# A linear-attention and MLP kernel: the order of norms in layer 0's first stage, and where four small loads are issued

## The chip, the core and the metric

The kernel runs on one core of a Trainium2 chip. The metric is the device time of one execution in microseconds (us); lower is better. The core has five engines with a queue of instructions each: TensorE (PE in the profile; PEld is its weight load, which overlaps the matmuls), VectorE (DVE), ScalarE (ACT), GpSimd (POOL) and SyncE (SP). Each engine takes its own queue strictly in order, and engines wait for each other through semaphores. In this kernel every DMA is issued from SP, so SP's queue is also the order in which transfers start: one transfer that must wait holds back all that stand behind it.

## The reference

Two layers, each a linear-attention block and a gelu MLP, both with a residual. All data is float32; S = 2048 rows, D = 448, 16 heads of 28, F = 1792.

```python
phi = lambda t: jnp.where(t > 0, t + 1, jnp.exp(t)) + 1e-6
pq, pk = phi(q), phi(k)                        # q, k, v = layernorm(x) @ wqkv
kv = jnp.einsum("bhsd,bhse->bhde", pk, v)
z = jnp.einsum("bhsd->bhd", pk)
num = jnp.einsum("bhqd,bhde->bhqe", pq, kv)
den = jnp.einsum("bhqd,bhd->bhq", pq, z)[..., None] + 1e-6
x = x + (num / den) @ wo
x = x + gelu(layernorm(x) @ w1 + b1) @ w2 + b2     # and both lines once more
```

Since kv and z are sums over all rows, the keys of all 2048 rows have to be through before the first row of the attention's output can be made.

## The kernel before

**Tiles.** The 2048 rows are 16 tiles of 128 rows. Products keep float32 accuracy by a split: each operand is rounded to a high part, the rest is a low part, and three matmuls (high by high, high by low, low by high) add up in one PSUM bank. That is why one projection of one tile is 11 matmuls of 448 columns, and why each tile needs a high part (ACT copies: `XH`, `xnh`, `kh`) and a low part (DVE or POOL subtracts: `XL`, `xnl`, `kl`).

**The first stage of a layer** (`phase1`, line 547) runs steps t = 1 to 15 in layer 0 (tile 0 and part of tile 1 are done in `launch`). A step is a string of tokens, read from left to right; the string is the order in which instructions enter the engines' queues, since the kernel writes its own schedule. The tokens stand for:

- `K`, `Q`, `G` (PE): the key projection of tile t, its query projection, and the product of the normed x of tile t-1 with its keys, added up over all tiles. From t = 9 on the queries are left for later, so a step is then 22 matmuls.
- `T`, `X`: tile t+1 turned so that its columns lie on the partitions, and its split. Tiles 0 to 5 are turned by PE (`T`, line 246). Tiles 6 to 15 go by way of DRAM: DVE turns them in squares of 32 (`turn`, lines 277 and 278), SP writes two tiles at a time to DRAM (`store_sq`, line 283) and reads them back in another order with four DMAs (`spread`, line 289); `X` then splits what landed (ACT line 295, DVE line 296).
- `a`, `n`: statistics of a tile (three DVE instructions, lines 193, 199 and 201, and `brs`, a power on POOL, line 203) and the norm itself (DVE line 383). `tu` and `tv` turn it, and after an odd tile store the pair. `sp` reads the pair back, `ld` issues the load of a later tile (line 82).
- `kp`, `kh`, `kl`: phi of the keys (ACT lines 317 and 318, DVE line 320), their high part (ACT line 433), low part and sum (DVE lines 440 and 444). `qp` and `q1` are the same phi for queries, with a store to DRAM (line 462). `s` splits the normed x for `G` (ACT line 415, POOL lines 416 and 417).
- `bg`: the MLP weights w1 and w2 are loaded and split in the background, a piece or two a step. A piece's load on SP (lines 91 to 94 for w1, 349 for w2) goes into one of two staging buffers and waits until POOL has finished with the piece that had the buffer (lines 342, 345, 353).

Which tiles are normed in which step stands in `NORM` (line 507), steps with an order of their own in `STEPS` (line 502).

**Other loads of the first stage.** After step 4 SP loads the biases b1 and b2 (lines 603 and 604), after step 11 wv (`stage_square`, lines 114 to 118), after step 13 wo (`trans_load`, line 616).

**The stage behind it** is written out in `ORDER` (line 494). It first reads back the queries of block 0 (`ld`, line 690: phi(q) from DRAM, and x, line 82), multiplies them with z on POOL (`qz`, line 694), makes kv out of `G` and wv (`kv`, line 641), divides the queries (`qs`, DVE lines 700 to 705), turns them (`tq`, PE line 712) and multiplies kv with wo (`m`, line 651). Query projections that were left over (`Q`) stand between these on PE.

After that come the MLP blocks (`mlp1`, `mlp2`), where PE runs without a break, and layer 1 in the same manner.

Of the kernel before, what the change touches and what calls it, by code (L numbers as in the profile page):

```python
# [22 lines left out]
def linear_attn_mlp_kernel(  # L23
# [15 lines left out]
    S, D = x0.shape  # L39
# [5 lines left out]
    G = 112  # L45
# [235 lines left out]
    def store_sq(key, h):  # L281
        d = stored[key, h] = dram([128, 1024], F32, f"sq_{'_'.join(map(str, key))}_{h}")
        sp.dma_start(d, squares.pop((key, h)))

    def spread(key, h):
        r = spreads[key, h] = half("sp")
        d = stored.pop((key, h)).rearrange("(i r) (m f) -> m r i f", i=4, m=4)
        for m in range(4):
            sp.dma_start(r[m * 32:(m + 1) * 32].rearrange("r (i f) -> r i f", i=4), d[m])
# [66 lines left out]
    bg = bg_pieces()  # L356
# [32 lines left out]
    def stage_t(l, t):  # L389
        if t >= TURNED[l]:  # L390
            turn(xns[l, t], ("a", l, t // 4), t % 4)
            if t % 2:
                store_sq(("a", l, t // 4), t % 4 // 2)

    def stage_sp(l, t):
        if t >= TURNED[l]:
            block(("a", l, t // 4))
            spread(("a", l, t // 4), t % 4 // 2)
# [76 lines left out]
    def stage_g(l, t, acc):  # L475
# [16 lines left out]


    ORDER = (
# [3 lines left out]
    )  # L498
    DEFER = NT - sum(tok in ("Q", "Qa") for tok in ORDER.split())

    STEP = "qp K T X s a kp n kh kl tu tv G bg Q ld sp"
    STEPS = {
# [3 lines left out]
    }  # L506
    NORM = (
        ((2,), (3,), (5, 6), (7,), (8,), (9,), (10,), (11,), (12, 13), (14,), (15,)),
        ((5,), (6,), (7,), (8,), (9,), (10,), (11,), (12, 13), (14,), (15,)),
    )  # L510

# [35 lines left out]
    def phase1(l, tr):  # L547
        za = consts.tile([128, D], F32, name="za", tag="za")
        acc = []
        load_to(l, 4 if l == 0 else NORM[l][1][-1])  # L550
        if l == 0:
            launch(za)
            load_to(l, NORM[l][2][-1])
        for t in range(l == 0, NT):
            norm = NORM[l][t] if t < len(NORM[l]) else ()
            for tok in STEPS.get((l, t), STEP).split():
                if tok[1:].isdigit() and tok[0] in "an":
                    (stage_a if tok[0] == "a" else stage_n)(l, int(tok[1:]))
                elif tok == "q1":
                    stage_qphi(1)  # L560
                elif tok == "sp":
                    for u in norm:
                        if u % 2:
                            stage_sp(l, u)
                elif tok == "ld" and t + 2 < len(NORM[l]):
                    load_to(l, NORM[l][t + 2][-1])
                elif tok == "a":
                    for u in norm:
                        stage_a(l, u)
                elif tok == "n":  # L570
                    for u in norm:
                        stage_n(l, u)
                elif tok == "tu":
                    for u in norm[:1]:
                        stage_t(l, u)
                elif tok == "tv":
                    for u in norm[1:]:
                        stage_t(l, u)
                elif tok == "T" and t + 1 < NT:
                    stage_b(l, t + 1, "acc" if t == 1 else "h")  # L580
                elif tok == "X" and t + 1 < NT and (l == 0 or t + 1 >= 4):
                    stage_x(l, t + 1)
                elif tok == "K":
                    stage_k(l, t)
                elif tok == "qp":
                    stage_qphi()
                elif tok == "kp":
                    stage_kphi(l, t)
                elif tok == "kh":
                    stage_kh(l, t)  # L590
                elif tok == "kl":
                    stage_kl(l, t, za)
                elif tok == "s":
                    stage_s(l, t)
                elif tok == "G" and t >= 1:
                    acc = acc or [bank("acc", 4, f"G{c}")[:, :D] for c in range(4)]
                    stage_g(l, t - 1, acc)
                elif tok == "bg" and l == 0:
                    background(BG[t])
                elif tok == "Q" and t < DEFER:  # L600
                    stage_q(l, t)
            if l == 0 and t == 4:
                sp.dma_start(b1s, b1.rearrange("(c p) -> p c", p=128))
                sp.dma_start(b2b, b2[None, :].to_broadcast([128, D]))
            if t == 11:
                tr.wv = stage_square(wqkv[:, 2 * D:])
            if t == 13:
                trans_load(l, tr)
        return za, acc

# [308 lines left out]
    for l in range(LAYERS):  # L919
        tr = SimpleNamespace(mp={})  # L920
        za, acc = phase1(l, tr)
        if l == 0:
            background(0)
        fill = list(range(DEFER, NT))

        def pre(j):
            for k in range(4):
                load_pq(l, 1, k)
            if l == 0:
                background(2)  # L930

        tok_ = SimpleNamespace(
            Q=lambda j: stage_q(l, fill.pop(0)), Qp=lambda j: fill_qphi(), Qv=lambda j: stage_qphi(j or 9),
            Qa=lambda j: stage_q(l, fill.pop(0), tag="acc"), G=lambda j: stage_g(l, NT - 1, acc),
            ld=lambda j: (load_pq(l, 0, j), load_x(l, j)), z=lambda j: trans_z(tr, za), gt=lambda j: trans_gt(tr, acc),
            kv=lambda j: trans_kv(tr), mask=lambda j: trans_mask(tr), m=lambda j: trans_m(tr, j),
            ms=lambda j: trans_ms(tr, j), qz=lambda j: q_z(l, 0, j, tr), qs=lambda j: q_scale(l, 0, j, tr),
            tq=lambda j: q_transpose(l, 0, j), qq=lambda j: q_split(l, 0, j), o=lambda j: o_mm(l, 0, j, tr),
            la=lambda j: o_ln(l, 0, j), lb=lambda j: o_n(l, 0, j), T=lambda j: m_transpose(l, 0, j),
            x=lambda j: m_split(l, 0, j), tu=lambda j: turn(xns.pop(("m", l, j)), ("m", l, 0), j),  # L940
            st=lambda j: store_sq(("m", l, 0), 0), sp=lambda j: spread(("m", l, 0), 0), pre=pre)
        for tok in ORDER.split():
            name, j = tok.rstrip("0123456789"), int("0" + tok.lstrip("abcdefghijklmnopqrstuvwxyzQTG"))
            getattr(tok_, name)(j)
        assert not fill and not qo
        table(AF.Gelu_apprx_tanh)
        q_z(l, 1, 0, tr)
        mlp1(l, 0, 0)
        trans_chunks(tr)
        for b in range(NB):  # L950
            acc = [bank("acc", 4, f"y{j}")[:, :D] for j in range(4)]
            nxt = b + 1 < NB
            if not nxt and l + 1 < LAYERS:
                st_k = stage_square(wqkv[:, D:2 * D])
                st_q = stage_square(wqkv[:, :D])
                load_to(l + 1, PRE - 1)
            for i in range(NF):
                if i + 1 < NF:
                    mlp1(l, b, i + 1)
                elif nxt:  # L960
                    mlp1(l, b + 1, 0)
                if l == 0 and b == 0 and i:
                    background(1, 1)
                if i == NF - 2 and not nxt and l + 1 < LAYERS:
                    table(AF.Exp)
                if 9 <= i < 13:
                    add_bias(l, b, i - 9)
                if nxt:
                    behind(l, b, i, tr)
                elif l + 1 < LAYERS:  # L970
                    if i == 2:
                        split_kq("k", st_k)
                    if i == 5:
                        split_kq("q", st_q)
                    if i in (3, 4, 6, 7, 8):
                        t = (3, 4, 6, 7, 8).index(i)
                        stage_a(l + 1, t)
                        stage_n(l + 1, t)
                        stage_t(l + 1, t)
                        if t % 2:  # L980
                            stage_sp(l + 1, t)
                    if 9 <= i < 13:
                        stage_x(l + 1, i - 9)
                mlp2(l, b, i, acc)
# [28 lines left out]
```

## Time and profile before

| | |
|---|---|
| time, median of 3 runs | 882.93 us (882.04 to 883.28) |
| the profiled execution | 880.54 us |
| its span, first to last instruction | 878.8 us |
| granted TensorE clock | 1.000 |
| busy, DVE / ACT / POOL | 489.9 / 342.7 / 220.6 us |
| DMA | 95.81 MB, mean 109 GB/s |

The profile gives busy times per engine, the instructions in order of time, a chain of waits that is followed back from a chosen end, and the DMAs. Matmuls are pipelined: one is shown with about 0.37 us while the next starts 0.20 to 0.21 us later, so a stall of PE is read from the distance of two starts and not from its busy time. In the rows, `out<-in` names the tile written and the tiles read; the bracket at a row's end is idle time of the engine just before it and what ended it. `SPq` rows are DMAs at the time when SP issues them. In the chain of waits a DMA's row starts at its issue and lasts until its data has landed.

### The profile page before, as it was taken

The numbers are of one execution on the slowest core, as the hardware profiler recorded it, in microseconds if no ns is written. First come the engines' busy times: TensorE is split into PE (matmuls) and PEld (weight loads), VectorE is DVE, ScalarE is ACT, GpSimd is POOL, SyncE is SP. The second block draws the span as 40 slices with busy tenths as digits, with TensorE's granted clock in tenths as the row PEclk, the third lists the DMA queues.
The fourth block names the chain that finished last, engine by engine and source line by source line (L and its number), as shares of the span: only waits on it lengthen the run. The fifth ranks groups of instructions, "written<-read, shape, count | busy, mean of one in ns | idle before, by whom it ended". The sixth has DMA issues, their size and how long they took to land.

```text
span 878.8 us, 11689 instructions
## 1 busy us (share of the span) xinstructions
PE 872.6 (99%) x4174; PEld 770.4 (88%) x4174; DVE 489.9 (56%) x957; ACT 342.7 (39%) x601; POOL 220.6 (25%) x250
## 2 busy tenths in 40 slices
PE   9999999999999999999999999999999999999998
PEld 8898888888888888888899998888888888888887
DVE  6878586658455544225567875864574473432112
ACT  6666645323223231333355665442233133223221
POOL 5466732325012102012222244220220140140000
PEclk9999999999999999999999999999999999999999
DMA  5476716624312502051135543262332323111001
GB/s 158 136 211 215 228 53 221 189 80 144 132 59 97 163 0 97 1 179 48 48 129 185 168 138 95 97 189 89 104 115 91 123 68 127 49 48 42 1 1 43
DMA packets 64202, 95.81 MB, mean 109 GB/s; under 512 B 8976, under 2 KB 59152, under 8 KB 64144
## 3 DMA queue, kind: packets, MB, share of 16 engines
q1 hardware_dynamic: 64144, 95.06, 34.3%
q8 instruction: 33, 0.54, 0.3%
q14 instruction: 25, 0.20, 0.1%
HBM read 56.70 MB, written 35.13 MB: 104 GB/s over the span
## 4 chain that ended last, share of the span: by engine, by line
PE 89%; DMA 4%; DVE 3%; ACT 1%; SPq 1%; issue 1%; POOL 1%; ACTq 0%; POOLq 0%; DVEq 0%
PE y L821 10%; PE y L820 10%; PE y L819 10%; PE hp L802 9%; PE hp L801 9%; PE hp L803 9%; PE hp L804 3%; PE hp L805 3%; PE psq L308 2%; PE psq L306 2%; PE psq L307 2%; PE op L744 2%; PE op L743 2%; PE op L745 2%; DMA sq_a<-sq 1%; DMA sp<-sq_a 1%
## 5 line engine op out<-in xcount | busy, mean ns | idle before, releaser
L811 DVE TENSOR_TENSOR gl<-g,gh 128x512 fp32r<-128x512 f32 x112 | 82.7, 738 | 300.2 <-ACT gh L810 300.2
L807 ACT ACTIVATE g<-hp,b1s 128x512 f32<-128x512 f32 x112 | 77.1, 689 | 406.5 <-PE hp L805 404.5
L821 PE MATMUL y<-w2h,gl 128*128 128x448 f32 x448 | 163.7, 365 | 0.0
L820 PE MATMUL y<-w2l,gh 128*128 128x448 f32 x448 | 163.6, 365 | 0.0
L819 PE MATMUL y<-w2h,gh 128*128 128x448 f32 x448 | 163.6, 365 | 0.0
L802 PE MATMUL hp<-XH,w1l 128*128 128x512 f32 x336 | 131.5, 391 | 0.0
L801 PE MATMUL hp<-XH,w1h 128*128 128x512 f32 x336 | 131.2, 391 | 0.0
L803 PE MATMUL hp<-XL,w1h 128*128 128x512 f32 x336 | 131.2, 391 | 0.0
L203 POOL TENSOR_TENSOR brs<-bve,mhalf 128x1 f32<-128x1 f32 x64 | 38.9, 609 | 279.1 <-DVE bve L201 275.9
L819 PEld LDWEIGHTS y<-w2h,gh 128*128 128x128 f32 x448 | 84.1, 188 | 9.0
L820 PEld LDWEIGHTS y<-w2l,gh 128*128 128x128 f32 x448 | 84.1, 188 | 8.4
L821 PEld LDWEIGHTS y<-w2h,gl 128*128 128x128 f32 x448 | 84.2, 188 | 6.6
L803 PEld LDWEIGHTS hp<-XL,w1h 128*128 128x128 f32 x336 | 63.1, 188 | 14.3 <-issue 0.6
L802 PEld LDWEIGHTS hp<-XH,w1l 128*128 128x128 f32 x336 | 63.1, 188 | 11.2
L801 PEld LDWEIGHTS hp<-XH,w1h 128*128 128x128 f32 x336 | 63.1, 188 | 10.9
L810 ACT CAST gh<-g 128x512 fp32r<-128x512 f32 x112 | 69.6, 622 | 3.6
L694 POOL TENSOR_TENSOR pz<-pq,zb 128x448 f32<-128x448 f32 x32 | 36.7, 1150 | 83.6 <-DVE dn L700 66.8
L416 POOL TENSOR_TENSOR xnl<-x,xnh 128x384 fp32r<-128x384 f32 x32 | 35.4, 1107 | 76.4 <-ACT xnh L415 48.3
L296 DVE TENSOR_TENSOR XL<-sp,XH 128x512 fp32r<-128x512 f32 x52 | 45.4, 879 | 10.7 <-ACT XH L295 10.7
L805 PE MATMUL hp<-XL,w1x 128*128 128x512 f32 x112 | 43.6, 389 | 0.0
L804 PE MATMUL hp<-XH,w1x 128*128 128x512 f32 x112 | 43.6, 389 | 0.0
L763 POOL TENSOR_TENSOR x<-x,b2b 128x448 f32<-128x448 f32 x32 | 41.9, 1332 | 0.0
(146 smaller groups left out, 1560.5 us busy)
## 6 DMA issues: line engine op xcount, KB each, us to landing
x<-in_A_x_dram SPq DMA_DIRECT2D x32, 224.0 KB, 3.8
pq_d<-eq SPq DMA_DIRECT2D x32, 224.0 KB, 2.9
pq<-pq_d SPq DMA_DIRECT2D x32, 224.0 KB, 3.3
sq_m<-sq SPq DMA_DIRECT2D x14, 512.0 KB, 2.8
sp<-sq_m SPq DMA_DIRECT2D x56, 128.0 KB, 2.9
x<-x_d SPq DMA_DIRECT2D x32, 224.0 KB, 3.3
sq_a<-sq SPq DMA_DIRECT2D x13, 512.0 KB, 2.9
sp<-sq_a SPq DMA_DIRECT2D x52, 128.0 KB, 3.0
```

Source lines behind the costliest of these rows:

```text
L296: eng.tensor_tensor(lo.rearrange("p (c i n) -> p c i n", c=4, n=32), x, f(h), op=OP.subtract)
L801: pe.matmul(o, w1h[:, c, s], x.moving(x.hi, c), start=(c == 0), stop=False)
L802: pe.matmul(o, w1l[:, c, s], x.moving(x.hi, c), start=False, stop=False)
L803: pe.matmul(o, w1h[:, c, s], x.moving(x.lo, c), start=False, stop=False)
L804: pe.matmul(o, w1x[:, s], x.moving(x.hi, 3), start=False, stop=False)
L805: pe.matmul(o, w1x[:, s], x.moving(x.lo, 3), start=False, stop=True)
L807: act.activation(g, hp, AF.Gelu_apprx_tanh, bias=b1s[:, i:i + 1])
L810: act.copy(gh, g)
L811: dve.tensor_sub(gl, g, f(gh))
L819: pe.matmul(acc[j], gh[:, s], w2h[:, i], start=first, stop=False)
L820: pe.matmul(acc[j], gh[:, s], w2l[:, i], start=False, stop=False)
L821: pe.matmul(acc[j], gl[:, s], w2h[:, i], start=False, stop=last)
```

## The change

All but the loads of wv and wo concerns layer 0 alone. In steps 1 to 3 the norm of tile 3 moves ahead of the second query phi, and the norm and turning of tile 6 move from step 2 to step 3. Tiles 12 to 15 were normed in steps 8 (12 and 13), 9 and 10, each wholly within its step; now the statistics, the norm and the turning of these tiles are put in separate places of steps 7 to 11. The statistics of tile 12 go to the end of step 7, ahead of `bg`; the turning and store of tiles 14 and 15 go behind `kp` of steps 10 and 11. Tile 12 is loaded one step earlier (`ld` of step 5). `sp` now reads back whatever pair is stored and not yet read. The loads of wv and wo are issued two steps later, and those of the biases move to the `ORDER` stage, behind the last `ld`. No arithmetic is added or removed.

```diff
     ORDER = (
-        "Q ld1 z ld0 ld2 qz0 qz1 G gt qs1 Q Qp kv qs0 tq1 Q mask qz2 tq0 qs2 ld3 "
+        "Q ld1 z ld0 ld2 qz0 qz1 G gt qs1 Q Qp kv qs0 tq1 Q mask qz2 tq0 qs2 ld3 b "
...
-    STEP = "qp K T X s a kp n kh kl tu tv G bg Q ld sp"
+    STEP = "qp K T X s a kp n kh kl tu G bg Q ld sp"
     STEPS = {
-        (0, 1): "T X a3 q1 s kh q1 n3 kl G bg ld sp",
-        (0, 2): "K T X s a4 kp n4 a5 kh kl n5 a6 n6 tv G bg Q ld sp",
+        (0, 1): "T X a3 q1 s kh n3 kl q1 G bg ld",
+        (0, 2): "K T X s a4 kp n4 a5 kh kl n5 a6 G bg Q ld",
+        (0, 3): "qp K T X s n6 v6 kp a7 kh kl n7 v7 G bg Q ld sp",
+        (0, 7): "qp K T X s a11 kp n11 kh kl v11 a12 G bg Q ld sp",
+        (0, 8): "qp K T X s a13 kp n12 kh kl v12 n13 v13 G bg Q ld sp",
+        (0, 9): "qp K T X s a14 kp n14 kh kl G bg",
+        (0, 10): "K T X s a15 kp v14 kh kl G bg",
+        (0, 11): "K T X s n15 kp v15 kh kl G bg sp",
         (1, 0): "K T X s kp kh kl a n tu Q ld sp",
     }
     NORM = (
-        ((2,), (3,), (5, 6), (7,), (8,), (9,), (10,), (11,), (12, 13), (14,), (15,)),
+        ((2,), (3,), (5, 6), (7,), (8,), (9,), (10,), (11, 12), (13,), (14,), (15,)),
...
-                if tok[1:].isdigit() and tok[0] in "an":
-                    (stage_a if tok[0] == "a" else stage_n)(l, int(tok[1:]))
+                if tok[1:].isdigit() and tok[0] in "anv":
+                    {"a": stage_a, "n": stage_n, "v": stage_t}[tok[0]](l, int(tok[1:]))
...
                 elif tok == "sp":
-                    for u in norm:
-                        if u % 2:
-                            stage_sp(l, u)
+                    for key, h in list(stored):
+                        block(key)
+                        spread(key, h)
...
-            if l == 0 and t == 4:
-                sp.dma_start(b1s, b1.rearrange("(c p) -> p c", p=128))
-                sp.dma_start(b2b, b2[None, :].to_broadcast([128, D]))
-            if t == 11:
+            if t == 13:
                 tr.wv = stage_square(wqkv[:, 2 * D:])
-            if t == 13:
+            if t == 15:
                 trans_load(l, tr)
...
+        def biases(j):
+            if l == 0:
+                sp.dma_start(b1s, b1.rearrange("(c p) -> p c", p=128))
+                sp.dma_start(b2b, b2[None, :].to_broadcast([128, D]))
```

The lines with `t == 13` and `t == 15` run in both layers, so that wv and wo are loaded two steps later in layer 1 as well.

More of the change, by code (lines that the diff above doesn't have):

```diff
@@ L573, in phase1 @@
                 elif tok == "tu":
[L574 to L577, printed above, removed]
+                    for u in norm:
                         stage_t(l, u)
@@ L940, in linear_attn_mlp_kernel @@
             x=lambda j: m_split(l, 0, j), tu=lambda j: turn(xns.pop(("m", l, j)), ("m", l, 0), j),
-            st=lambda j: store_sq(("m", l, 0), 0), sp=lambda j: spread(("m", l, 0), 0), pre=pre)
+            st=lambda j: store_sq(("m", l, 0), 0), sp=lambda j: spread(("m", l, 0), 0), pre=pre, b=biases)
         for tok in ORDER.split():
```

## The prediction

> **What bounds the kernel now.** I read the busy times first, then PE's rows in order of time for the first 130 us (the only stretch whose order changes much), then the chain of waits there, and last DVE, POOL, SP and ACT around each stall.
>
> ```profile
> PE 872.6 (99%) x4174; PEld 770.4 (88%) x4174; DVE 489.9 (56%) x957; ACT 342.7 (39%) x601; POOL 220.6 (25%) x250
> ```
>
> PE works through nearly the whole span, and the change adds and removes no matmul and leaves PE's order as it is. So the time can move only by PE's stalls, and those of layer 0's first stage are few:
>
> ```profile
> 22.36 0.37 PE L311 MATMUL psk<-wk,XL 128*128 128x448 f32 x1
> 23.08 0.55 PE L246 MATMUL tp<-ident,x 128*128 128x128 f32 x3 [0.34 <-DVE x L383]
> ...
> 32.85 0.37 PE L485 MATMUL G<-kl,xnh 128*128 128x448 f32 x1
> 33.29 0.47 PE L306 MATMUL psq<-wq,XH 128*128 128x448 f32 x1
> ...
> 73.57 0.36 PE L484 MATMUL G<-kh,xnh 128*128 128x448 f32 x1
> 73.77 0.37 PE L485 MATMUL G<-kl,xnh 128*128 128x448 f32 x1
> 74.55 0.47 PE L306 MATMUL psk<-wk,XH 128*128 128x448 f32 x1 [0.41 <-ACT XH L295]
> ...
> 77.42 0.48 PE L481 MATMUL G<-kh,xnh 128*128 128x448 f32 x1
> 78.08 0.47 PE L482 MATMUL G<-kl,xnh 128*128 128x448 f32 x1 [0.18 <-DVE kl L440]
> ...
> 98.85 0.36 PE L307 MATMUL psk<-wk,XH 128*128 128x448 f32 x1
> 99.23 0.47 PE L308 MATMUL psk<-wk,XL 128*128 128x448 f32 x1
> ...
> 101.24 0.47 PE L481 MATMUL G<-kh,xnh 128*128 128x448 f32 x1
> 101.90 0.47 PE L482 MATMUL G<-kl,xnh 128*128 128x448 f32 x1 [0.19 <-DVE kl L440]
> ```
>
> Two matmuls that don't wait start 0.20 us apart (73.57, 73.77). Distances less 0.20 are the stalls: 0.52 us at the turning of tile 3, 0.24 at the query projection of step 3, 0.58 where the keys of tile 10 wait for their split XH, 0.46 at the G product behind it, 0.18 at the keys of tile 15 and 0.46 at the G product there. That is 2.4 us; beside a few smaller ones it is all that a better order can give here.
>
> The stall at 74.55 is a DMA's. The chain of waits shows a loop: two tiles are turned, stored, read back, split; and DVE and ACT, in order behind that split, then norm and turn the next pair.
>
> ```profile
> 56.19 3.42 DMA sp<-sq_a
> ...
> 65.10 3.11 DMA sq_a<-sq
> ...
> 69.54 4.23 DMA sp<-sq_a
> ...
> 73.88 0.63 ACT XH L295
> ```
>
> The reader is to see that tiles 10 and 11 were stored at 65.10, read back from 68.2 on, and landed at 73.77; PE had come to their keys at about 73.97. Whatever PE gains before that point is gone there, unless this landing moves too.
>
> **The change part by part.** *Steps 1 to 3.* The norm of tile 3 no longer stands behind a query phi that waits for ACT, and that of tile 6 no longer holds up step 3's query phi and split.
>
> ```profile
> 21.98 0.62 DVE L320 SCALAR_TENSOR_TENSOR eq<-psq,eq 128x448 f32<-128x448 f32 x1 [0.93 <-ACT eq L318]
> ...
> 31.41 0.51 DVE L383 TENSOR_SCALAR x<-x,bmv,brs 128x448 f32<-128x448 f32 x1 [0.73 <-POOL brs L203]
> ```
>
> Both stalls of PE go, 0.52 + 0.24 = 0.76 us. On DVE the two idle times, 0.93 + 0.73 = 1.66 us, can be filled, so that the pair 6 and 7, and with it the loop, comes at most 1.66 us earlier. I take 1.3, since the split of tile 4 still waits for PE. PE's own 0.76 us are worth nothing by themselves: they lengthen the wait at 74.55.
>
> *Tile 12 loaded in step 5* puts one more load of 128 x 448 x 4 B = 229 KB on SP ahead of the read-back of tiles 8 and 9.
>
> ```profile
> 50.00:60.00 10.00, 10.00 (x52) 9.26 (x51) 7.70 (x17) 6.84 (x14) 6.77 (x7) 1.00 0.83 253
> ```
>
> At the 253 GB/s of that stretch it costs 0.9 us of transfer. So the pair 8 and 9, and the turning of tile 11 that follows, is 1.3 - 0.9 = 0.4 us earlier.
>
> *Statistics of tile 12 at the end of step 7, ahead of bg.* This is the step I count as the most costly. What stands there:
>
> ```profile
> 64.81 0.27 DVE L278 STREAM_TRANSPOSE sq<-x 128x128 f32<-128x128 f32 x1
> ...
> 67.60 0.62 DVE L193 BATCH_NORM_STATS2 bst<-x 128x6 f32<-128x448 f32 x1
> ...
> 68.46 0.15 DVE L201 TENSOR_SCALAR bve<-bmv 128x1 f32<-128x1 f32 x1
> ```
> ```profile
> 63.79 1.16 POOL L345 TENSOR_TENSOR w1x<-stg,w1x 64x448 fp32r<-64x448 f32 x1 [1.06 <-ACT w1x L344]
> 65.03 1.16 POOL L342 TENSOR_TENSOR w1l<-stg,w1h 128x448 fp32r<-128x448 f32 x1
> ...
> 68.70 0.55 POOL L203 TENSOR_TENSOR brs<-bve,mhalf 128x1 f32<-128x1 f32 x1 [0.30 <-DVE bve L201]
> ```
> ```profile
> 66.03 0.83 SPq L91 DMA_DIRECT2D stg<-in_B_w_dram  x2
> 66.92 0.44 SPq L82 DMA_DIRECT2D x<-in_A_x_dram  x1
> 68.22 2.36 SPq L289 DMA_DIRECT2D sp<-sq_a  x4
> ```
>
> In the changed order POOL takes the power of tile 12 (brs) ahead of the two weight subtractions, and that power needs DVE's three statistics, which now stand behind the turning of tile 11. The turning ends at 64.81 + 0.27 = 65.08, now 64.7; statistics 1.0 (67.60 to 68.61) make 65.7; the power starts 0.1 later and takes 0.55: 66.3, where the first subtraction had started at 63.79. The second ends 2.40 us after the first starts (66.19 - 63.79): 68.7 for 66.19. The two weight loads on SP wait for just these subtractions, and behind them on SP stand the load of tile 14 and the read-back of tiles 10 and 11. So the second weight load is issued at 68.8, the load at 69.3, the read-back from 69.75 on at 0.45 each, its last DMA at 71.1 for 69.54. With the 3.42 to 4.23 us that a read-back took from there it lands between 74.5 and 75.3, against 73.77: 0.7 to 1.5 us later. I take +1.0 us at the keys of tile 10, since fewer transfers are in flight by then. Lower bound: all 1.66 us gained, the load of tile 12 free, 3.42 us to land: -0.5 us; upper bound +1.5.
>
> *Tiles 14 and 15.* The turning of tile 15 goes behind the key phi of step 11.
>
> ```profile
> 83.86 2.91 DMA sq_a<-sq
> ```
> ```profile
> 85.11 0.62 DVE L320 SCALAR_TENSOR_TENSOR psk<-psk,ek 128x448 f32<-128x448 f32 x1
> ```
> ```profile
> 92.21 0.62 ACT L295 CAST XH<-sp 128x512 fp32r<-128x512 f32 x1
> ...
> 95.05 0.64 ACT L433 ACTIVATE kh<-psk,tiny 128x448 fp32r<-128x448 f32 x1 [0.70 <-DVE psk L320]
> ```
> ```profile
> 94.19 0.36 PE L306 MATMUL psk<-wk,XH 128*128 128x448 f32 x1
> ...
> 96.42 0.36 PE L481 MATMUL G<-kh,xnh 128*128 128x448 f32 x1
> ```
>
> The store at 83.86 comes after that phi's 0.62 and a turning of 0.7: about 86.2, 2.3 us later. Store, issues and landing take 2.91 + 1.35 + 3.42 = 7.7 us, so the split of tile 14 starts at 93.9 for 92.21, 1.7 later, and the high part of tile 13's keys, behind it on ACT, ends at 95.69 + 1.7 = 97.4 where G wants it at 96.42. That is a new stall of 1.0 us (0.4 to 1.5). Against it, wv is no longer ahead of the last w1 piece, for which ACT waited before the split of tile 15, so 0.18 + 0.46 = 0.64 us of stalls go. Net +0.4, from -0.2 to +0.9.
>
> *wv and wo two steps later.* wv is now sent just ahead of w2's pieces, wo and the first queries; the kv product has cover for it, the queries don't.
>
> ```profile
> 100.00:110.00 10.00, 9.81 (x46) 8.28 (x45) 5.25 (x8) 6.11 (x12) 7.58 (x10) 1.00 0.91 282
> ```
> ```profile
> 108.53 2.27 POOL L694 TENSOR_TENSOR pz<-pq,zb 128x448 f32<-128x448 f32 x2
> ```
> ```profile
> 112.04 0.63 DVE L705 SCALAR_TENSOR_TENSOR pq<-pq,rd 128x448 f32<-128x448 f32 x1
> ```
> ```profile
> 114.62 0.60 PE L712 MATMUL tq<-ident,pq 128*112 128x128 f32 x4
> ```
>
> wv is (448 + 64) x 448 x 4 B = 918 KB. The DMA engines are 0.91 busy there at 282 GB/s: 3.25 us in which queries land later, POOL's two products with z start later, and DVE's division ends at 112.67 + 3.25 = 115.9, for the turning on PE at 114.62. The cover is 1.95 us, the stall 1.3; I take +1.2, with bounds 0 (wv goes out while SP waits for staging buffers) and +2.2 (wo's two issues, now between the last w2 piece and the queries, add 0.9). [...]
>
> *The biases* leave the middle of step 4 and go behind the queries' loads. The attention of block 0 hides them ahead of the first gelu; without that cover PE would wait a whole landing. Layer 1 loads wv and wo later too, but sends no weight pieces in that stage; I count nothing.
>
> Sum: +1.0 + 0.4 + 1.2 = +2.6 us. Against the profiled execution's 880.54 that is 883.1; this execution was 2.4 below the median of the runs, 882.93, from which I forecast 885.5.
>
> **The rivals.** *The stalls simply go* (0.16): the read-back of tiles 10 and 11 lands at least 0.8 us earlier, PE gains 0.76 + 0.58 + 0.46 before step 11 and 0.64 behind: -2.4, 880.5. For it speaks that 1.66 us of DVE's idle time lie on the loop; against it, that SP's queue holds the read-back behind loads that wait for POOL. It decides at 66.46, when the second weight load went out: if that stays, this is what happens.
>
> *Gain and loss cancel* (0.23): the landing keeps its 73.77 and wv goes out in gaps, +0.4 or less is left: 883.1.
>
> *Everything at its upper bound* (0.18): 1.5 + 0.9 + 2.2 = +4.6, 887.5. For it speaks that each delay also pushes w2's pieces, on which SP waits again.
>
> The forecast has 0.43.
>
> **How the numbers follow.** The forecast's own range is 882.4 to 887.5 (-0.5 to +4.6). For 8 in 10 I widen it to 881.2 to 888.2. A measurement of this kernel tells about 0.2%, 1.8 us, from no change. Slower by more: most of the forecast and the upper case, 0.60. Within: the cancelling case and the forecast's lower edge, 0.23. Faster: 0.17.
>
> **What would show it.** Right: the turning of tile 3 without a gap; the second weight load of step 7 near 68.8 and the read-back behind it; a longer wait of tile 10's keys (over 1.5 us); a wait for kh before G of step 14; none at tile 15; a wait of the first tq. Wrong: the read-back issued at 68 or earlier, or PE at the end of step 15 ahead of before.

## The result, and the profile after

The changed kernel takes 890.50 us (median of 5 runs, 889.92 to 891.41), the kernel before 882.04 us in the same series (881.32 to 883.28): a ratio of 1.0095, with a 95% interval of 1.0080 to 1.0110. It is 8.4 us slower. The forecast was 2.6 us slower, so the direction held and the size was a third of what came.

The profiled execution after spans 889.3 us against 878.8. PE's rows after, in order of time, at the places where the prediction showed those of before:

```profile
22.25 0.37 PE L311 MATMUL psk<-wk,XL 128*128 128x448 f32 x1
22.46 0.49 PE L246 MATMUL tp<-ident,x 128*128 128x128 f32 x3
...
32.26 0.36 PE L306 MATMUL psq<-wq,XH 128*128 128x448 f32 x1
...
74.21 0.37 PE L485 MATMUL G<-kl,xnh 128*128 128x448 f32 x1
78.75 0.74 PE L306 MATMUL psk<-wk,XH 128*128 128x448 f32 x1 [4.17 <-ACT XH L295]
...
81.15 0.58 PE L306 MATMUL psk<-wk,XH 128*128 128x448 f32 x1
81.53 0.58 PE L307 MATMUL psk<-wk,XH 128*128 128x448 f32 x1
...
101.94 0.47 PE L481 MATMUL G<-kh,xnh 128*128 128x448 f32 x1
...
107.24 0.37 PE L482 MATMUL G<-kl,xnh 128*128 128x448 f32 x1
...
123.39 0.65 PE L712 MATMUL tq<-ident,pq 128*112 128x128 f32 x4 [3.01 <-DVE pq L705]
...
126.32 0.57 PE L308 MATMUL psq<-wq,XL 128*128 128x448 f32 x1
126.69 0.57 PE L310 MATMUL psq<-wq,XH 128*128 128x448 f32 x1
```

Both stalls of steps 1 to 3 are gone: the turning of tile 3 starts 0.21 us behind the matmul ahead of it, and the queries of step 3 come 1.03 us sooner (32.26 for 33.29). Then it turns round. Tile 10's keys start at 78.75 for 74.55, 4.20 us late; G of step 14 at 101.94 for 96.42, 5.52 late; the G product that before had waited at 101.90 comes at 107.24, 5.34 late; and the first tq at 123.39 for 114.62, 8.77 late. Behind both long waits neighbouring matmuls start 0.37 to 0.38 us apart (81.15, 81.53; 126.32, 126.69) and not 0.20. At the end it is 10.5 us in these two executions. No other stage loses anything of note.

What held tile 10's keys is seen on three queues of the changed kernel. First POOL:

```profile
67.81 0.55 POOL L203 TENSOR_TENSOR brs<-bve,mhalf 128x1 f32<-128x1 f32 x1 [3.41 <-DVE bve L201]
68.44 1.40 POOL L345 TENSOR_TENSOR w1x<-stg,w1x 64x448 fp32r<-64x448 f32 x1
69.91 1.16 POOL L342 TENSOR_TENSOR w1l<-stg,w1h 128x448 fp32r<-128x448 f32 x1
```

then SP:

```profile
66.78 0.33 SPq L283 DMA_DIRECT2D sq_a<-sq  x1
69.86 1.80 SPq L91 DMA_DIRECT2D stg<-in_B_w_dram  x2
71.72 0.42 SPq L82 DMA_DIRECT2D x<-in_A_x_dram  x1
72.18 1.86 SPq L289 DMA_DIRECT2D sp<-sq_a  x4
```

POOL stands idle for 3.41 us until the statistics of tile 12 are ready, and only then subtracts w1; SP's two loads of line 91 wait for that; the read-back of tiles 10 and 11 stands behind them. It starts 5.40 us behind the store of the pair (72.18 less 66.78), before it was 3.12 (68.22 less 65.10).

And the new thing, on DVE and POOL in steps 1 to 3. DVE's rows and then POOL's, of the changed kernel:

```profile
21.11 1.19 DVE L383 TENSOR_SCALAR x<-x,bmv,brs 128x448 f32<-128x448 f32 x1 [0.20 <-POOL brs L203]
...
32.16 1.12 DVE L383 TENSOR_SCALAR x<-x,bmv,brs 128x448 f32<-128x448 f32 x1
...
36.51 1.08 DVE L383 TENSOR_SCALAR x<-x,bmv,brs 128x448 f32<-128x448 f32 x1
```
```profile
21.04 1.01 POOL L416 TENSOR_TENSOR xnl<-x,xnh 128x384 fp32r<-128x384 f32 x1
...
32.01 1.02 POOL L416 TENSOR_TENSOR xnl<-x,xnh 128x384 fp32r<-128x384 f32 x1 [0.77 <-ACT xnh L415]
...
36.19 1.15 POOL L342 TENSOR_TENSOR w1l<-stg,w1h 128x448 fp32r<-128x448 f32 x1
```

The norm took 0.50 to 0.52 us in this stage of the kernel before, where none started inside a subtraction of POOL. Moved, it does and takes 1.08 to 1.19. In all three cases it ends 0.25 us behind POOL's instruction: 22.05, 33.03 and 37.34 end POOL's, 22.30, 33.28 and 37.59 the norms. So the norm's end hangs on POOL's end. Why it does, and why only 0.25 of the norm's 0.51 us come behind it, no run shows.

The trace of the kernel before held this cost already, in layer 1, beyond the 130 us that the prediction read. DVE, then POOL:

```profile
452.70 1.21 DVE L383 TENSOR_SCALAR x<-x,bmv,brs 128x448 f32<-128x448 f32 x1 [0.73 <-POOL brs L203]
```
```profile
452.63 1.02 POOL L416 TENSOR_TENSOR xnl<-x,xnh 128x384 fp32r<-128x384 f32 x1
```

This norm comes just behind its `brs`, but POOL has begun a subtraction 0.07 us before it, and the norm ends 0.26 us behind that subtraction's end (453.91 for 453.65).

Last, the clock. The windows of the changed kernel; the columns are the window, its length, PE's busy time and instructions, the granted TensorE clock, the DMA share and GB/s:

```profile
73.30:76.70 3.40, 1.27 (x7) 1.00 0.87 262
76.70:80.10 3.40, 1.35 (x4) 0.50 0.91 314
80.10:83.50 3.40, 3.40 (x11) 0.50 0.75 213
...
121.00:124.40 3.40, 1.01 (x7) 1.00 0.34 95
124.40:127.80 3.40, 3.40 (x12) 0.51 0.75 162
```

In the stretches from 73.30 and 121.00 on, in which PE works 1.27 and 1.01 us, nothing is seen yet; the next 3.4 us are granted 0.50 and 0.51 of the clock, and at tile 10 those behind them too (from 83.5 on it is 1.00 again). By the pace of 0.37 to 0.38 us for 0.20, I estimate that one such stretch costs at most half of itself, 1.7 us; less where PE would have waited in it anyway.

### The profile page after: what moved, and what is told of

The parts are those of the page before. It is cut to its first block, busy times and chain, and to the rows that moved or that the text cites. A ratio compares the mean times of both kernels' runs of the same rounds, so it can differ in the third digit from the quotient of the medians.

```text
span 889.3 us, 11689 instructions
## 1 busy us (share of the span) xinstructions
PE 876.4 (99%) x4174; PEld 773.5 (87%) x4174; DVE 492.2 (55%) x957; ACT 342.9 (39%) x601; POOL 220.3 (25%) x250
## 4 chain that ended last, share of the span: by engine, by line
PE 86%; DVE 0%; issue 0%; DVEq 0%
PE y L821 10%; PE y L819 10%; PE y L820 10%; PE hp L802 9%; PE hp L801 9%; PE hp L803 9%; PE hp L805 3%; PE hp L804 3%; PE op L744 2%; PE op L743 2%; PE op L745 2%; PE psq L306 1%; PE psq L308 1%; PE psq L307 1%; PE psk L307 1%; PE G L481 1%
```

## Experiments

A ratio is to the kernel before, in runs on the same chip, with its 95% interval; 0.0010 is 0.9 us. A trace is one execution. That of the kernel before, 880.54 us, is a quick one of its kind (the medians were 880.9 to 882.9), and 12 of 17 other traces lose some 0.6 us at an early product of the first MLP block (`hp`, for `XL`) where it doesn't. So a lateness against it is compared up to the first tq, and the price of a part is taken from the ratios.

**Parts undone.** wv and wo back at their old steps:

```diff
-            if t == 13:
+            if t == 11:
                 tr.wv = stage_square(wqkv[:, 2 * D:])
-            if t == 15:
+            if t == 13:
                 trans_load(l, tr)
```

> The changed kernel with the loads of wv and wo back behind steps 11 and 13. Theory: wv stands ahead of the queries in the DMA engines, and that alone makes the first turning of queries wait 3.0 us; the low clock behind that wait goes with it. PE's lead over the kernel before, +10.5 us at the end, stays at the +5.5 us that it had at the z product: 885.6 us, no wait at the first tq. Rival: the queries are late because w2's pieces are late on POOL, whatever wv does: the wait stays at 1 to 3 us and the time above 888.

Measured 1.0071 (1.0051 to 1.0091): 2.1 us of the 8.4 go, not 4.9, and the interval overlaps the changed kernel's. The run with the filled gap below, which has wv and wo back as well, has no wait at the first tq, but PE is 8.0 us late at the product for z already, where the changed kernel was 5.5. The statistics of tile 12 back in step 8:

```diff
-        (0, 7): "qp K T X s a11 kp n11 kh kl v11 a12 G bg Q ld sp",
-        (0, 8): "qp K T X s a13 kp n12 kh kl v12 n13 v13 G bg Q ld sp",
+        (0, 7): "qp K T X s a11 kp n11 kh kl v11 G bg Q ld sp",
+        (0, 8): "qp K T X s a12 a13 kp n12 kh kl v12 n13 v13 G bg Q ld sp",
```

> The changed kernel with the statistics of tile 12 back in step 8; tile 12 is still loaded in step 5. Theory: POOL subtracts the w1 pieces of step 7 at once, SP is free for the read-back of tiles 10 and 11 about 2.3 us earlier (near 70 us), tile 10's keys wait under 2.5 us instead of 4.2 and the matmuls behind that wait run at full pace: 3.7 us less at step 10, 886 to 888 us at the end. Rival: it is the load of tile 12 and the crowded DMA engines: the read-back goes out near 70 but lands late all the same, the wait stays over 3.5 us, 889.5 or more.

Measured 1.0094 (1.0073 to 1.0115): as the changed kernel. SP's rows of this run, then PE's:

```profile
67.97 0.33 SPq L283 DMA_DIRECT2D sq_a<-sq  x1
...
70.93 2.44 SPq L289 DMA_DIRECT2D sp<-sq_a  x4
...
76.58 0.34 SPq L283 DMA_DIRECT2D sq_a<-sq  x1
```
```profile
77.19 0.47 PE L306 MATMUL psk<-wk,XH 128*128 128x448 f32 x1 [1.42 <-ACT XH L295]
...
98.27 0.47 PE L306 MATMUL psk<-wk,XH 128*128 128x448 f32 x1 [0.87 <-ACT XH L295]
...
122.39 0.65 PE L712 MATMUL tq<-ident,pq 128*112 128x128 f32 x4 [3.28 <-DVE pq L705]
```

The queue of waits is as it was thought: with the statistics gone the read-back follows its store by 2.96 us, and tile 10's keys wait 1.42 in place of 4.17. But the next pair is stored at 76.58 (74.61 in the changed kernel, 72.41 before): its norms come behind one more set of statistics, 0.94 us on DVE, and tile 13's norm now starts inside a subtraction of w1 and takes 1.26 us. Tile 14's keys wait 0.87; and the first tq waits 3.28. What one wait gives up the next ones take.

Steps 1 to 3 back:

```diff
-        (0, 1): "T X a3 q1 s kh n3 kl q1 G bg ld",
-        (0, 2): "K T X s a4 kp n4 a5 kh kl n5 a6 G bg Q ld",
-        (0, 3): "qp K T X s n6 v6 kp a7 kh kl n7 v7 G bg Q ld sp",
+        (0, 1): "T X a3 q1 s kh q1 n3 kl G bg ld",
+        (0, 2): "K T X s a4 kp n4 a5 kh kl n5 a6 n6 v6 G bg Q ld",
+        (0, 3): "qp K T X s a7 kp n7 kh kl v7 G bg Q ld sp",
```

> The changed kernel with steps 1 to 3 as before. Theory: the norms of tiles 3, 6 and 7 run beside a long subtraction on POOL and take 1.1 us for 0.5; put back they take 0.5 again, the pair 6 and 7 is stored at 37.9 for 38.4, and PE comes 0.8 us later to tile 10's keys: the wait is 2.8 to 3 us for 4.2. If a wait of that length is short enough for the clock, 888.5; if not, 890. Rival: these steps are a gain as they were meant, then putting them back costs 0.5 to 1 us: 891 or more.

Measured 1.0080 (1.0061 to 1.0098): 1.3 us better than the changed kernel by the ratios, with intervals that overlap. So this part, which was meant to bring time, brings none in sight here, and may cost some.

**Is it the clock?** As the first experiment, with matmuls on a constant in the place where PE would stand:

```diff
             norm = NORM[l][t] if t < len(NORM[l]) else ()
+            if l == 0 and t == 10:
+                fill_in = bank("h", 2, "fill")
+                for i in range(14):
+                    pe.matmul(fill_in[:, :128], ones, ones, start=True, stop=True)
```

> The first of these kernels (wv and wo back) with 14 matmuls of 128 columns on constants put ahead of tile 10's keys; their result is not used, and they take about 3 us inside the wait of 4.2. Theory: the 13 matmuls at 0.37 us pace behind that wait are a lower clock that the wait itself brings; with PE kept at work the clock stays at 1.0, they run at 0.20, and the time is 1.4 us below the kernel without them. Rival: the slow matmuls have another cause (late operands, crowded memory): same time or slower, and they stay at 0.37.

Measured 1.0083 (1.0064 to 1.0102): not faster than without them. The windows of this run:

```profile
80.00:82.00 2.00, 1.94 (x9) 1.00 0.62 197
...
98.80:102.20 3.40, 1.80 (x8) 1.00 1.05 312
102.20:105.60 3.40, 3.40 (x11) 0.51 0.32 78
```

With the gap filled the clock stays at 1.00 behind tile 10's wait (0.50 in the changed kernel): there it was the idle PE that lowered it. But no time is won. The timed runs of this kernel show mean clocks of 0.998 to 1.000 and are no faster for it; in the trace PE waits 1.54 us at tile 14's keys, and the clock falls there. So the half clock behind tile 10's wait has no price of its own that these runs can tell. That a later read-back would have held PE anyway fits this trace; it was not tested apart.

**Parts alone, in the kernel before.** Steps 1 to 3 as the change has them, all else as before:

> The kernel before with the new order of steps 1 to 3 alone (steps 7 to 11, biases, wv and wo as before). Theory A: the norms of tiles 3 and 6 (L383) stand beside the POOL subtractions L416 and take 1.1 to 1.2 us in place of 0.51, the pair 6/7 is stored 0.5 us later and not 1.3 us earlier, and tile 10's keys wait about 1.0 us longer than before: PE early by 0.8 us up to there, +1.0 us from there on, some 883 us against 882. The step of the forecast that is on record (pair 6/7 comes 1.3 us earlier): -0.8 us, 881.2, and no longer wait at tile 10.

Measured 1.0011 (1.0001 to 1.0020); the medians are the same, 881.94 us against 881.96. So there is no gain, and a loss between nothing and 1.8 us. The norms took 1.19 and 1.11 us, and tile 10's keys came 1.26 us later than before, but 0.52 of that stood in this execution before the first moved norm (the turning of tile 2, 18.14 for 17.62). And it isn't kept: tile 15's keys and the G product behind them no longer wait, and at the first tq PE is 0.32 us late. The theory has its sign; its size isn't shown. The same with the split moved out of the norms' way:

```diff
-        (0, 1): "T X a3 q1 s kh n3 kl q1 G bg ld",
+        (0, 1): "T X s a3 q1 kh n3 kl q1 G bg ld",
...
-        (0, 3): "qp K T X s n6 v6 kp a7 kh kl n7 v7 G bg Q ld sp",
+        (0, 3): "qp K T X n6 v6 kp s a7 kh kl n7 v7 G bg Q ld sp",
```

> As e5_only_steps123, with the split of the inputs (s) ahead of the statistics in step 1 and behind norm and turn of tile 6 in step 3, so that no norm stands beside an L416 subtraction of POOL. Theory A: the norms of tiles 3 and 6 take 0.51 us again, the pair 6/7 comes earlier than in e5, tile 10's wait is no longer than before: 0.5 us under before, 881.4, and 1.5 us under e5. Rival, that the long norms are not what makes the pair late: the same as e5 within 0.3 us.

Measured 1.0001 (0.9992 to 1.0010), 881.44 us. DVE's rows of the norms of tiles 3, 6 and 7:

```profile
21.09 0.51 DVE L383 TENSOR_SCALAR x<-x,bmv,brs 128x448 f32<-128x448 f32 x1 [0.21 <-POOL brs L203]
...
31.61 0.51 DVE L383 TENSOR_SCALAR x<-x,bmv,brs 128x448 f32<-128x448 f32 x1
...
35.34 1.09 DVE L383 TENSOR_SCALAR x<-x,bmv,brs 128x448 f32<-128x448 f32 x1
```

Tiles 3 and 6, out of POOL's way, take 0.51 again; tile 7, which still meets a subtraction of w1, takes 1.09. That settles what makes a norm long. What it is worth at the end, 0.9 us by the ratios, is not settled: the intervals overlap. And the long norms are not all that stood against the gain. Here the pair 6 and 7 is stored 0.60 us earlier than before (37.27 for 37.87), but the last of its four reads takes 4.96 us for 4.09, the split behind it starts 0.19 us later (46.64 for 46.45), and tile 10's keys come 0.74 us later. What slowed that read no run separates.

wv and wo alone:

> The kernel before with wv loaded in step 13 and wo in step 15 (norms, steps 1 to 3 and biases as before). Theory A: the first transposing of the queries (tq) waits for pq, TensorE stands there, +1.6 us, 883.5; if that wait comes to about 3 us the clock falls behind it and another 1.5 us goes (885). Rival, that in the changed kernel the wait at tq stems from the late read-back of tiles 14 and 15 alone and not from wv's place: no change, 882, and no wait at tq.

Measured 1.0037 (1.0023 to 1.0051). PE's row of the first tq in this run:

```profile
116.08 0.65 PE L715 MATMUL tq<-ident,pq 128*112 128x128 f32 x4 [1.59 <-DVE pq L708]
```

The read-back of the queries among the DMAs of 98 to 108 us in this run; the last column is the median time from issue to landing:

```profile
pq<-pq_d SPq DMA_DIRECT2D x3, 224.0 KB, 6.2
```

and the same row of the kernel before:

```profile
pq<-pq_d SPq DMA_DIRECT2D x3, 224.0 KB, 4.0
```

The first of these reads is issued only 1.0 us later than before (104.39 for 103.41); they land 2.2 us later still, behind wv. In the changed kernel they take 7.3 us. So the wait at tq is the doing of this part, and here it is 1.59 us with all else as before. In the timed runs the mean clock was 0.996 to 0.999, where the kernel before had mostly 1.000: in some of them this wait probably brought the clock down too.

The load of tile 12 alone:

```diff
-        ((2,), (3,), (5, 6), (7,), (8,), (9,), (10,), (11,), (12, 13), (14,), (15,)),
+        ((2,), (3,), (5, 6), (7,), (8,), (9,), (10,), (11, 12), (13,), (14,), (15,)),
```

> The kernel before with the inputs of tile 12 loaded in step 5 and nothing else changed. Theory A: the transfer lies ahead of the read-back of tiles 8/9, which takes 1.2 us longer to land (4.6 us for 3.4), tile 10's pair is turned and stored 1.2 us later, and the keys of tile 10 wait that much longer: +1.2 us at the end, 882.1 against 880.9. Rival, that the whole cost of the strewn norm lies in its place on VectorE and POOL and not in this load: no change, and the landing stays at 3.4 us.

Measured 1.0015 (1.0005 to 1.0024), 1.3 us. The read-back of tiles 8 and 9 among the DMAs of 50 to 62 us in this run:

```profile
sp<-sq_a SPq DMA_DIRECT2D x4, 128.0 KB, 4.9
```

and in the kernel before:

```profile
sp<-sq_a SPq DMA_DIRECT2D x4, 128.0 KB, 3.4
```

In the changed kernel, whose four reads follow their store by the same 3.0 us as before, it took 4.6. So it is not a later issue on SP that costs; what is new ahead of the four reads is the transfer of tile 12. The biases alone:

> The kernel before with the two biases loaded behind the first loads of the queries and nothing else changed. Theory A (the forecast on record): no change, within 0.3 us. Rival: step 4's transfers of the biases (0.42 and 1.63 us of SP's time in the kernel before) stand before those of tiles 8/9, and without them tile 8's keys come up to 0.5 us sooner: 880.5; or, at the new place, they hold up the fourth read-back of the queries and the end comes 0.5 us later.

Measured 0.9997 (0.9988 to 1.0006): nothing, as forecast.

**The strewn norm.** All of it (statistics, load of tile 12, biases), with steps 1 to 3, wv and wo as before:

> The changed kernel with steps 1 to 3 and the places of wv and wo as before: what is left of the change is the strewn norm (with the load of tile 12 a step earlier) and the late biases. Theory A: the keys of tile 10 wait some 3.5 us longer than before, with TensorE at half clock for 3.4 us behind it where the wait fills most of such a stretch, the step of tile 14 brings another +0.9, and the end is 4.5 to 5.5 us above before (886.5 to 887.5). If the three parts simply add (0.9 and 2.7 to 3.3 us were measured for the other two alone, 8.4 for all), it is 4.2 to 4.8 us: 886 to 887. Rival, that the strewn norm costs only what the forecast on record gave it (1.9 us): 884.

Measured 1.0063 (1.0049 to 1.0078), 886.44 against 880.89. The same with tile 12's statistics back:

> As e9_only_norms, with the statistics of tile 12 in step 8 again and not at the end of step 7 (its load stays in step 5). Against e9 this is the price of the early statistics without the late queries to swallow it. Theory A: POOL is free for w1 when the pair 10/11 is stored, the read-back starts 3 us behind the store and not 5.4, the keys of tile 10 wait 2 us less, the clock stays: 2 to 3 us under e9 (884.5). Rival (transfers, not POOL, hold the read-back): as e9 within 0.5 us. Second rival: the wait moves to tile 14's keys and half of it is kept, 1 us under e9.

Measured 1.0060 (1.0041 to 1.0079), 885.56: by the medians 0.9 us less, by the ratios 0.3. The first theory's 2 to 3 us is wrong. In the trace the wait moves, as the second rival had it (1.69 us at tile 10's keys for 3.23, and 0.69 at tile 14's); by its time the first rival, no change, isn't excluded. The changed kernel with steps 9 to 11 as before:

```diff
-        (0, 9): "qp K T X s a14 kp n14 kh kl G bg",
-        (0, 10): "K T X s a15 kp v14 kh kl G bg",
-        (0, 11): "K T X s n15 kp v15 kh kl G bg sp",
+        (0, 9): "qp K T X s a14 kp n14 kh kl v14 G bg",
+        (0, 10): "K T X s a15 kp n15 kh kl v15 G bg sp",
+        (0, 11): "K T X s kp kh kl G bg",
```

> The changed kernel with steps 9 to 11 as before, so that norm and turn of tiles 14 and 15 are no longer strewn. Theory A: the wait at the keys of tile 10 (4.2 us) stays, the new wait at tile 14's keys goes, the queries still wait behind wv: 0.9 us under the changed kernel (889.6). Rival, that what is lost here is taken over by the wait at the first tq anyway: no change (890.5), and a longer wait at tq.

Measured 1.0087 (1.0069 to 1.0104): some 0.7 us less, not told apart from none. There is no wait left at tile 14's keys, and still 2.48 us at the first tq, for which wv is enough. Then the strewn norms of tiles 12 to 15 alone in the kernel before, with load and statistics where they were, and last only step 8 of it:

> The kernel before with norm and turn of tiles 12 to 15 strewn over steps 8 to 11 as in the changed kernel, but with tile 12 loaded and its statistics taken where the kernel before has them. Theory A: tile 13's norm, now behind the turn of tile 12, and tile 15's norm a step later make the pairs 12/13 and 14/15 late by 1.5 and 5 us, tile 14's keys wait 1 to 2 us: +2.5 us, 883.8, which with the 1.3 us of the early load and the 0.3 to 0.9 us of the early statistics gives the 5.5 us of the whole norm part. Rival, that the strewing costs nothing by itself where the early load is gone: 881.3.

> As e16_strewn_without_load12, with steps 9 to 11 as before: tile 13's norm and turn behind tile 12's is all that is left. Theory A: the pair 12/13 is stored about 1.5 us later, which the slack ahead of tile 12's keys takes up in part, +0.5 us, 881.8; e16 less this is the price of the strewn tiles 14 and 15, about 2 us. Rival: tile 13's place makes all of it, as e16.

Measured 1.0030 (1.0019 to 1.0041) and 1.0005 (0.9996 to 1.0014). So tiles 14 and 15 make 2.2 us. DVE's, SP's and PE's rows of the first of the two:

```profile
84.93 1.20 DVE L383 TENSOR_SCALAR x<-x,bmv,brs 128x448 f32<-128x448 f32 x1
86.06 0.62 DVE L320 SCALAR_TENSOR_TENSOR psk<-psk,ek 128x448 f32<-128x448 f32 x1
```
```profile
87.38 0.33 SPq L283 DMA_DIRECT2D sq_a<-sq  x1
...
90.30 1.75 SPq L289 DMA_DIRECT2D sp<-sq_a  x4
```
```profile
95.97 0.47 PE L306 MATMUL psk<-wk,XH 128*128 128x448 f32 x1 [1.16 <-ACT XH L295]
...
102.11 0.47 PE L306 MATMUL psk<-wk,XH 128*128 128x448 f32 x1 [0.31 <-ACT XH L295]
```

Tile 15's norm is another long one (1.20 beside POOL); the key phi and the turning follow behind it; the pair is stored at 87.38 for 83.86, 3.5 us late, and tiles 14 and 15 both wait.

**A faster one.** Read-back ahead of the next load in the kernel before (and step 1 as in the run with the split moved):

```diff
+        (0, 3): "qp K T X s a7 kp n7 kh kl v7 G bg Q sp ld",
+        (0, 4): "qp K T X s a kp n kh kl tu G bg Q sp ld",
...
+        (0, 8): "qp K T X s a12 a13 kp n12 n13 kh kl v12 v13 G bg Q sp ld",
...
-            if t == 11:
+            if t == 12:
```

> The kernel before with the read-back of the keys (sp) ahead of the load of the next inputs (ld) in steps 3 to 8 of layer 0, the input split ahead of the statistics in step 1, and wv one step later. Theory A (what the keys of tile 10 wait for is the read-back queued on SP behind loads that nobody needs yet): the read-backs come 0.5 to 1 us sooner, the wait of tile 10 shrinks, 880.5, 1.4 us under before. Rival, that the read-back is held by the transfers themselves and not by its place in SP's queue: 882, as before; or the inputs come late for the statistics and it is slower than before.

Measured 1.0017 (1.0008 to 1.0026), slower. Tile 10's split starts 0.8 us sooner, but the pair 14/15 is stored 0.8 us later, since tile 15 is loaded late, and from 0.07 us late at the G product of step 15 PE goes to 1.3 us late at the product for z. With step 8 and wv put back:

> As e8_readback_first, with the load ahead of the read-back again in step 8 (so that tile 15 comes in time) and wv in step 11 as before. Theory A: e8 lost its gain at the late load of tile 15 (+0.8) and at wv one step later (+1.3); without both, tile 10's keys come 0.6 us sooner and nothing later gives it back: 881.2, 0.6 us under before. Rival, that the read-back of the queries or the transfers behind tile 10 take the gain: 882, as before.

Measured 0.9990 (0.9981 to 0.9999). With the biases late as well:

> As e11_readback_first_to_step7, with the biases at their late place: whether this part of the change is worth keeping in the fastest version found. Theory A: the same as e11 within 0.3 us, 0.6 to 0.9 us under before. Rival: 0.5 us less or more than e11, from SP's time in step 4 or at the new place.

Measured 0.9985 (0.9976 to 0.9994), 879.99 us against 881.26: the fastest here, by 1.3 us. PE at tile 10's keys in this run:

```profile
73.02 0.37 PE L485 MATMUL G<-kl,xnh 128*128 128x448 f32 x1
73.27 0.47 PE L306 MATMUL psk<-wk,XH 128*128 128x448 f32 x1
```

The wait at which the kernel before lost 0.58 us is 0.05 now (0.25 between the two starts, of which 0.20 is the pace).

## Why the prediction was wrong

Its own terms against what was measured for each part alone (the price by its ratio, 0.0010 as 0.9 us):

| part | forecast, us | alone, us |
|---|---|---|
| steps 1 to 3 | gain, up to 1.3 for the loop | +1.0 (0.1 to 1.8), by the medians 0 |
| tile 12 loaded in step 5 | +0.9, covered by that gain | +1.3 (0.4 to 2.1) |
| tile 12's statistics in step 7 | +1.0 at tile 10's keys | +0.3 to +0.9, not told from none |
| tiles 14 and 15 (and 13) strewn | +0.4 | +2.6 (1.7 to 3.6) |
| wv, wo | +1.2 | +3.3 (2.0 to 4.5) |
| biases | 0 | -0.3 (-1.1 to 0.5) |
| all | +2.6 | 8.4 (7.1 to 9.7) |

The parts alone come to 8.2 to 8.8 us. That this meets the whole is partly luck: the norm part as a whole took 5.6 us where its pieces make 4.2 to 4.8, and wv and wo, undone, gave back only 2.1 of their 3.3.

The forecast's sum had three terms, and each was some 2 us short: +1.0 at tile 10's keys (the first three rows alone make 2.6 to 3.2), +0.4 for tiles 14 and 15, +1.2 for wv and wo. In the first a step was wrong; the other two were mis-sized.

- *Steps 1 to 3: the step that failed.* "On DVE the two idle times ... can be filled, so that the pair 6 and 7 ... comes at most 1.66 us earlier. I take 1.3." The waits were filled, and PE's 0.76 us did go. But the norms were moved out of places where POOL was idle into POOL's subtractions, and three of them grew by 0.57 to 0.68 us. The pair was stored not 1.3 us earlier but 0.56 later (38.43 for 37.87), and the gain that was to cover the load of tile 12 fell away. Alone this part was to bring time and brought none (+1.0 us by the ratios, nothing by the medians). "And with it the loop" didn't hold either: where the pair did come 0.60 us earlier, the gain was gone in its read-back.
- *Tile 12's load:* right in its place and near in its size, 1.3 for 0.9. It isn't SP's time that costs: in the changed kernel the read-back follows its store by the same 3.0 us as before, and with this part alone it lands 1.5 us later (4.9 for 3.4).
- *Tile 12's statistics:* the mechanism was right in every link (the power ahead of w1 on POOL, the two loads of line 91, the read-back at 72.18 where 69.75 was forecast), and tile 10's wait came. Its forecast of where the loss ends was wrong: of the 2.3 us between store and read-back (5.40 less 3.12) less than 1 stays, since the wait moves on to later tiles. I called it the most costly step; it was the cheapest of the norm part.
- *Tiles 14 and 15:* mis-sized, +2.2 by the two runs where +0.4 stood. The store was put at 86.2 and came at 87.38 where this part stands alone: the working took the start of the key phi, 85.11, from before, and with tile 15's norm in front of it, 1.20 us long beside POOL, it starts at 86.06. The 0.64 us that tile 15 was to give back didn't come there, since its keys wait for the same late read-back. In the changed kernel it came (PE is 6.1 us late at tile 15's keys and 5.2 behind the first G products), but not by wv's place: with only steps 1 to 3 changed it comes as well (1.27 to 0.34).
- *wv and wo:* the mechanism, the place and the size of the first wait were right (+1.3 forecast, 1.59 measured alone). The term, +1.2, was too small by 2.1 us (by 1.5 if the medians are taken, 884.66 less 881.96). The trace shows 1.7 us of it, from 0.29 early at the product for z to 1.45 late at the first tq. Behind that PE loses 1.0 us more, but so it does where wv and wo stay (0.95 with only the biases late, 1.0 with only steps 1 to 3), so that is no price of theirs. What makes up the rest stays open; the lower clock in the timed runs may be part of it. The working took the 282 GB/s of a stretch of 10 us; in slices of 0.28 us the kernel before moves 365 to 404 GB/s from 107.4 to 109.0 us. By that rate the wait would have come out shorter still.
- *The clock* stood nowhere in the forecast. At tile 10 it cost nothing that could be told. At the first tq nothing takes it over: in the changed kernel PE goes from 8.77 us late there to 10.1 at the second tq (127.44 for 117.32); the run with tile 12's statistics back waited as long at this tq, 3.28 us, kept its clock and lost 0.1 on this way.

Of the signs named beforehand, tile 3 without a gap, the late read-back, the wait of tile 10's keys, none at tile 15 and the wait of the first tq are all in the trace after; the wait for kh at step 14 is not (0.19 us, for kl). So the chain of causes could be read, and its sizes could not. Of the rivals, "everything at its upper bound" (+4.6) was the nearest, and still 4 us short: the bounds of each term were drawn from rows of before, from a stage in which no norm started beside a subtraction of POOL and no wait reached 3 us. (The lower ends of its terms add up to -0.7, not to the -0.5 that it used.)

## What to carry to other kernels

Before an instruction is moved into idle time of its engine, look at what the other engines do there: a gap of DVE that held one of POOL's subtractions was no gap, since the norm took 1.08 us or more in it for 0.51. In a loop of store, read-back and split, a transfer that nobody needs yet can cost even where SP issues the read-back no later: tile 12's early load brought the four reads behind it from 3.4 to 4.9 us and cost 1.3; put the read-back ahead of loads that are not needed soon (ahead of tile 15's load it cost time). And take a part's price from that part alone: undone within a slow kernel, its loss is taken over by the next wait.

## What the hardware showed that was not expected

The granted clock goes to 0.50 for 3.41 us at a time (in the changed kernel twice in a row behind tile 10's wait, once behind that of the first tq), and the length of one wait does not decide whether it does. In the changed kernel it fell behind stretches of 3.4 us with 1.27 and 1.01 us of PE's work; in the run with the filled gap it fell behind one with 1.80, whose longest single wait was 1.54 us. And in the run with tile 12's statistics back a wait of 3.28 us left the clock alone:

```profile
117.60:121.00 3.40, 1.51 (x16) 1.00 0.16 59
121.00:124.40 3.40, 2.01 (x12) 1.00 0.60 185
```

(windows of that run, columns as above). That trace has no fall of the clock between 60 and 140 us, so it doesn't show where such stretches lie in it; however they are laid there, one of them holds some 1.77 us of PE's work or less (summed from windows of 0.1 us). So PE's busy time alone doesn't seem to decide it either, though by little: 1.77 us or less kept the clock here where 1.80 had lost it. What counts, these runs don't show. In the changed kernel the clock changes at 76.71, 83.54, 124.50 and 127.91 us: 6.83, 40.96 and 3.41 us apart, whole multiples of 3.41.
